# Dealing out the weight decoding, and moving a numerator copy, in linear attention with two MLPs

## The chip, the cores and the metric

The kernel runs on one core of one Trainium2 chip. The metric is device time in microseconds (us) of the whole launch; lower is better. Inputs are float32 (the MLP weights and alpha come as float64 and are split on the chip), and the output is float32.

## What is computed

```python
def phi(x):
    proj = np.einsum('bhsd,df->bhsf', x, w_phi)
    proj = proj - np.max(np.abs(proj), axis=-1, keepdims=True)
    return np.concatenate([np.exp(proj), np.exp(-proj)], axis=-1)
q_p, k_p = (phi(q), phi(k))
kv = np.einsum('bhsf,bhsd->bhfd', k_p, v)
z = np.sum(k_p, axis=2)
num = np.einsum('bhsf,bhfd->bhsd', q_p, kv)
den = np.einsum('bhsf,bhf->bhs', q_p, z)[..., None] + 1e-06
x = num / den                    # 4 batches, 8 heads, 576 tokens, 64 wide
h = x @ w_in1;  x = (h * np.cos(h)) @ w_out1
h = x @ w_in2;  x = (np.maximum(h, 0) + alpha * np.minimum(h, 0)) @ w_out2
```

The MLPs see 2304 tokens of 512 features, with 2048 hidden features.

## The kernel before, in words

**One order, written by hand.** The program is one list of steps, and every engine executes its instructions in the order in which the code issues them. Attention takes steps s = 0 to 50: eight groups n of four heads, five chunks of tokens each. In a step the tuple `order` calls its stages from top to bottom. The stages of a step work on different chunks: `project(s)` (TensorE, tile pj) makes the projections of key chunk s and of query chunk s - 2; `less_max` (VectorE, L460 and L464) takes the largest magnitude of a chunk and subtracts it; `k_exp` (ScalarE, L474) makes both exponentials of key chunk s - 1; `kv` (TensorE, L484) uses those of chunk s - 2; `q_transpose` (TensorE, L530, tile tp) and `q_exp` (ScalarE L549 and L563, GpSimd L565) make the query features as a high and a low part. This document counts steps by s, and calls s modulo 5 the remainder of the step.

**Numerators.** `num(n, pr, half, y)` multiplies query features by kv on TensorE (tile nm, L577) and copies the result out of PSUM in L583: with VectorE for y = 0, with ScalarE for y = 1. `NUM_AT` says in which step. Remainder 2, 3 and 4 have a numerator of either y, remainder 0 only one of y = 0, and remainder 1 only one of y = 1: that one is the lone numerator. nm and tp come in turn from one pool of two PSUM buffers, so a tile can only be written when the copy or the exponentials that read the tile two before it are done.

**Decoding.** The MLP weights are read as pairs of 32-bit words (`fetch_w`, two buffers ws) and turned into a high and a low float32r part by the ten instructions of `w_instructions`: ScalarE L118, L115 (the high part) and L129; VectorE L119, L123, L126, L127; GpSimd L132, L133, L134. The first five weights are decoded in attention (`w_some`, at the steps `W_AT`, parts spread by `W_PART`: L119 and L123 in the first step, L126 in the next, L127 after it). The others are decoded in the MLP steps k (`moe_step`), where a small planner picks the steps (`times`, `free`, `latest`, `decode_at`). MLP step k = -6 falls on s = 42, so the last attention steps and the first MLP steps share a time.

**MLP steps.** Step k computes one hidden tile (12 matmuls, ph), five steps ahead, and one output (12 matmuls, po) of a block of three or four hidden tiles; at the end of a block VectorE adds the four po tiles to acc (L236, L238), and only then the next block may write po. The last group of tokens has 256 tokens and two po tiles.

**Denominators.** `recip` sends a row to VectorE's layout and back through DRAM: transfers L592, L596 and L598 on SyncE's queue, `x_mult` (VectorE L605) uses what comes back, `x_split` (ScalarE L612, GpSimd L614) writes the MLP's input xh, xl.

Of the kernel before, what the change touches and what calls it, by code (L numbers as in the profile page):

```python
# [28 lines left out]
def feature_map_attention_two_mlps(  # L29
# [17 lines left out]
    NG4 = qT.shape[0]  # L47
# [46 lines left out]
    def w_instructions(spare=True):  # L94

        layer, which, ft, st = staged.pop(0)
        w_temps.append(w_temps.pop(0))
        u = w_temps[0].tile([P, DM], F32, tag="wu", name="wu")  # L100
        t = w_temps[0].tile([P, DM], I32, tag="wt", name="wt")
        e = w_temps[0].tile([P, DM], I32, tag="we", name="we")
        w0, w1 = st[:, :, 0], st[:, :, 1]
        tf, ef = t.bitcast(F32), e.bitcast(F32)
        ts, stt = nc.vector.tensor_scalar, nc.vector.scalar_tensor_tensor
        tt = nc.gpsimd.tensor_tensor
        tv, copy = (nc.vector.tensor_tensor, nc.vector.tensor_copy) if spare else (tt, nc.scalar.copy)
        hl = []

        def to_hi():  # L110
            hl.extend(w_tile(layer * NFT + ft, which, x) for x in "hl")
            w_t[layer, which, ft] = tuple(
                z.rearrange("p (k f) -> p k f", k=KD) if which == 0 else z for z in hl
            )
            copy(hl[0], tf)  # L115

        return [
            lambda: nc.scalar.activation(out=u, in_=w1.bitcast(F32), func=AF.Abs),  # L118
            lambda: ts(  # L119
                out=e, in0=w1, scalar1=0x07FFFFFF, scalar2=3, op0=ALU.bitwise_and,  # L120
                op1=ALU.logical_shift_left,
            ),
            lambda: stt(  # L123
                out=t, in0=w1, scalar=-0x40000000, in1=e, op0=ALU.bitwise_and, op1=ALU.bitwise_or
            ),
            lambda: stt(out=tf, in0=u, scalar=MIN_PATTERN, in1=tf, op0=ALU.is_ge, op1=ALU.mult),  # L126
            lambda: ts(out=e, in0=t, scalar1=-0x00800000, scalar2=None, op0=ALU.bitwise_and),  # L127
            to_hi,
            lambda: nc.scalar.activation(  # L129
                out=u, in_=w0.bitcast(U32), func=AF.Copy, scale=2.0 ** -52  # L130
            ),
            lambda: tt(out=u, in0=u, in1=ef, op=ALU.mult),  # L132
            lambda: tv(out=tf, in0=tf, in1=hl[0].bitcast(F32), op=ALU.subtract),  # L133
            lambda: tv(out=hl[1], in0=tf, in1=u, op=ALU.add),  # L134
        ]
# [17 lines left out]
    half_pi = const.tile([P, 1], F32, name="half_pi")  # L153
    al = const.tile([P, NFT], F32, name="al")
    h_t, g_t, o_t, pools = {}, {}, [], {}
    x_todo = []

    def mm3(ps, pairs, first=True, last=True):
        n = 3 * len(pairs)
        m = 0  # L160
        for (lh, ll), (rh, rl) in pairs:
            for l, r in ((lh, rh), (lh, rl), (ll, rh)):
                nc.tensor.matmul(ps, lhsT=l, rhs=r, start=(first and m == 0), stop=(last and m == n - 1))  # L163
                m += 1
# [50 lines left out]
    def output(j):  # L215
        layer, ft, g, fts = steps[j]
        c0, n = groups[g]
        gg = g_t.pop(j)
        ww = w_t[layer, 1, ft]
        nm = KD if layer == 0 else n // P  # L220
        w = n if layer == 0 else DM
        if ft == fts[0]:
            o_t[:] = [
                pools["ps_o"].tile([P, 512], F32, tag=f"po{m}", name=f"po{m}") for m in range(nm)
            ]
        for m in range(nm):
            s = slice(m * P, (m + 1) * P)
            l, r = (ww, gg) if layer == 0 else (gg, ww)
            mm3(o_t[m][:, 0:w], [((l[0][:, s], l[1][:, s]), r)], ft == fts[0], ft == fts[-1])
        if ft != fts[-1]:  # L230
            return
        for m in range(nm):
            po = o_t[m][:, 0:w]
            a = acc[g][:, m * w:(m + 1) * w]
            if fts[0] == 0:
                nc.vector.tensor_copy(a, po)  # L236
            else:
                nc.vector.tensor_tensor(out=a, in0=po, in1=a, op=ALU.add)  # L238
            if ft == NFT - 1:
                if layer == 0:  # L240

                    x_todo.append((xh[:, m, c0:c0 + n], xl[:, m, c0:c0 + n], a, nc.gpsimd))
                else:
                    nc.sync.dma_start(out=out[c0 + m * P:c0 + (m + 1) * P, :], in_=a)
# [21 lines left out]
    def reads(layer, which, ft):  # L266
        js = [j for j, st in enumerate(steps) if st[:2] == (layer, ft)]
        lead = LEAD_H - 1 if which == 0 else 0
        return js[0] - lead, js[-1] - lead

    w_all = []
    for i in range(2 * NFT):
        for which in range(2):
            w = (i // NFT, which, i % NFT)
            old = i - WSLOTS
            free = reads(old // NFT, which, old % NFT)[1] if old >= 0 else -1
            w_all.append((reads(*w)[0], free, w))
    w_all.sort(key=lambda w: w[0])
    w_seq = [w[2] for w in w_all[:len(EARLY)]]
# [1 line left out]
    def quiet(k):  # L281

        return (k < 0 or steps[k][1] != steps[k][3][-1]) and steps[k + LEAD][2] != NG - 1

    decode_at, at, todo = {}, -LEAD - 1, w_all[len(EARLY):]
    times = [t for t in range(1 - LEAD // 2, len(steps) - LEAD) if quiet(t)]
    latest = {}
    for need, free, w in reversed(todo):
        latest[w] = max(t for t in times if t < min([need - 2, *latest.values()]))
# [43 lines left out]
    with ExitStack() as actx:  # L333
# [286 lines left out]

        LAG = 2
        NUM_AT = (
            {5: (0, 0), 6: (0, 1), 7: (1, 0), 8: (1, 1)},
# [1 line left out]
        )  # L628
        NUM_LAST = 8
        KV_AT, KV_END, KV_LO = {5: (0,)}, {6: (1,)}, {5: (0,), 7: (1,)}  # L630
        W_AT = (7, 15, 23, 30, 37)
        W_PART = (0, 0, 0, 1, 2, 3, 3, 3, 4, 4)

        def num_step(n, pr, half, y):
            at = next(r for r, x in NUM_AT[y].items() if x == (pr, half))
# [17 lines left out]
                            f(n, pr, *a)  # L653
            return go

        w_run = []

        def w_some(s):
            if s in W_AT:
                w_run.extend(zip((s + d for d in W_PART), w_instructions(spare=False)))  # L660
            while w_run and s >= w_run[0][0]:
                w_run.pop(0)[1]()
                if not w_run:
                    fetch_w(*w_seq.pop(0))

# [7 lines left out]
        def group(f, table, lag, *a):  # L673
# [3 lines left out]
                        f(n, *table[s - lag - n * NC], *a)  # L677
            return go


        order = (
            group(kv_hi, KV_AT, 0),
            chunk(k_exp, -1, 0),
            chunk(kv, -2),
            nums_of(0),
            chunk(less_max, -LAG - 1, kind="q"),
            chunk(k_exp, -1, 1),
            nums_of(1),
            lambda s: kv_some(),
            group(kv_lo, KV_LO, 0),  # L690
            after(recip, 2, 2),
# [7 lines left out]
            chunk(q_exp, -LAG - 2, 1, True),  # L699
            after(x_split, 4, 5, False),  # L700
            after(x_split, 4, 5, True),
            w_some,
            chunk(less_max, 0, kind="k"),
        )


# [5 lines left out]
        for s in range(NS):  # L712
            if s + 3 < NK:
                load_x("k", s + 3)
                if s % NC == 2 and s // NC + 1 < NG4:
                    for pr in range(2):
                        load_v(s // NC + 1, pr)
            if 0 <= s - LAG + 3 < NK:
                load_x("q", s - LAG + 3)
            for stage in order:  # L720
                stage(s)
            if s < LAG:

                keep_warm(WARM)
            if s == 5:
                nc.sync.dma_start(
                    out=al, in_=alpha.rearrange("(f p) -> p f", p=P), allow_slow_non_contiguous=True
                )
            if s in (5, 7):
                fetch_w(*w_seq.pop(0))  # L730
            if s == S_H:
                kctx.close()
                pctx.close()
                pools["gp"] = ctx.enter_context(
                    tc.tile_pool(name="gp", bufs=LEAD + 1, reuse_waits="tile", side="right")
                )
                pools["mt"] = ctx.enter_context(
                    tc.tile_pool(name="mt", bufs=2, reuse_waits="tile", side="right")
                )
                pools["ps_h"] = ctx.enter_context(  # L740
                    tc.tile_pool(name="ps_h", bufs=4, space=PSUM, reuse_waits="tile")
                )
            if s == S_O:
                qctx.close()
                w_pools.append(ctx.enter_context(
                    tc.tile_pool(name="wpool2", bufs=1, reuse_waits="tile")
                ))
                w_temps.append(ctx.enter_context(
                    tc.tile_pool(name="wtmp2", bufs=1, reuse_waits="tile")
                ))  # L750
                pools["ps_o"] = ctx.enter_context(
                    tc.tile_pool(name="ps_o", bufs=1, space=PSUM, reuse_waits="tile", side="right")
                )
            if s >= S_H:
                assert not w_run and len(w_t) >= len(EARLY)
                moe_step(s - S_H - LEAD_H)
# [56 lines left out]
```

## Time and profile before

| what | value |
|---|---|
| median of 3 runs | 1007.64 us (1006.25 to 1009.91) |
| the profiled execution | 1009.28 us |
| its span, first to last instruction | 1007.1 us |
| mean granted TensorE clock | 0.993 |
| PE (matmul) busy | 985.2 us, 98% |
| DVE (VectorE) busy | 715.3 us, 71% |
| POOL (GpSimd) busy | 612.3 us, 61% |
| ACT (ScalarE) busy | 485.0 us, 48% |
| chain that ended last | PE 79%, DVE 11%, ACT 5%, issue 2%, DMA 1% |

A timeline row has its start, its length, the engine, the line, the operation, output<-input and the count; in brackets stands the idle time of that engine just before it, and what ended it. In a row of the waits stand the total, the number of waits and the longest. A windows row has its length, then the busy time of PE, PEld (weight loads), DVE, ACT and POOL with their instructions, the granted TensorE clock as a share of full speed, the DMA share and GB/s. PE's ends are modelled, so gaps in PE are read from the idle times, and lengths from start to start.

### The profile page before, as it was taken

Reading aid. Unit: us, or ns where it says so; the run is one execution under the profiler, and the core shown is the slowest. Engines: PE = TensorE matmul, PEld = TensorE weight load, DVE = VectorE, ACT = ScalarE, POOL = GpSimd, SP = SyncE. Lnnn points to the kernel's source line nnn. Section 1 sums busy time; section 2 is a strip of 40 time slices with the busy share of each in tenths; the row PEclk is TensorE's granted clock in tenths of the full one; section 3 lists DMA queues with packets and bytes.
Section 4 is the critical chain, followed back from the end, with each engine's and each line's share of the span. In section 5 each row is a group of like instructions: output and inputs, shape, how many; then the busy total and the mean of one; then the engine's idle time right before and its main releaser. Section 6 shows DMA issues by size and latency. Waiting matters only on the chain.

```text
span 1007.1 us, 14702 instructions
## 1 busy us (share of the span) xinstructions
PE 985.2 (98%) x5515; PEld 826.0 (82%) x5515; DVE 715.3 (71%) x1007; ACT 485.0 (48%) x935; POOL 612.3 (61%) x494
## 2 busy tenths in 40 slices
PE   9989989999999999999999999999999999999998
PEld 6988888877888888888888888888888888888887
DVE  5888878557785785885885788587749774976333
ACT  4868868775655654664656654223212321222000
POOL 2667768846474663663777789666636663676221
PEclk9989989999999999999999999999999999999999
DMA  6454443221020110110111111111101110110112
GB/s 155 131 134 130 116 138 95 65 68 43 21 64 22 63 42 21 63 42 21 63 63 43 31 54 43 42 43 56 50 21 42 63 44 21 42 63 1 42 42 105
DMA packets 64582, 60.67 MB, mean 60 GB/s; under 512 B 28928, under 2 KB 54656, under 8 KB 64512
## 3 DMA queue, kind: packets, MB, share of 16 engines
q1 hardware_dynamic: 64512, 59.75, 19.9%
q8 instruction: 43, 0.70, 0.3%
q14 instruction: 27, 0.22, 0.1%
HBM read 52.50 MB, written 4.79 MB: 57 GB/s over the span
## 4 chain that ended last, share of the span: by engine, by line
PE 79%; DVE 11%; ACT 5%; issue 2%; DMA 1%; POOL 1%; SPq 1%; ACTq 0%; DVEq 0%; POOLq 0%
PE po L163 34%; PE ph L163 33%; PE kv L484 4%; PE nm L577 4%; DVE wt L123 2%; PE pj L451 2%; DVE wt L126 2%; DVE we L119 1%; DVE r L190 1%; PE tp L530 1%; PE tp L416 1%; DVE acc L605 1%; DVE we L127 1%; DVE mx L460 1%; ACT r L193 1%
## 5 line engine op out<-in xcount | busy, mean ns | idle before, releaser
L86 POOL TENSOR_TENSOR gl<-r,gh 128x512 fp32r<-128x512 f32 (+1 forms) x160 | 207.5, 1298 | 274.2 <-ACT gh L85 255.2
L85 ACT CAST gh<-r 128x512 fp32r<-128x512 f32 (+1 forms) x160 | 92.0, 575 | 363.4 <-DVE r L209 260.5
L163 PE MATMUL ph<-xh,wil 128*128 128x512 f32 (+1 forms) x640 | 236.8, 370 | 0.1
L163 PE MATMUL ph<-xh,wih 128*128 128x512 f32 (+1 forms) x640 | 236.6, 370 | 0.0
L163 PE MATMUL ph<-xl,wih 128*128 128x512 f32 (+1 forms) x640 | 235.8, 368 | 0.0
L238 DVE TENSOR_TENSOR acc<-po,acc 128x512 f32<-128x512 f32 (+1 forms) x134 | 85.2, 656 | 75.6 <-PE po L163 75.2
L163 PEld LDWEIGHTS ph<-xl,wih 128*128 128x128 f32 x640 | 120.4, 188 | 22.1
L163 PEld LDWEIGHTS ph<-xh,wih 128*128 128x128 f32 x640 | 120.5, 188 | 21.9
L163 PEld LDWEIGHTS ph<-xh,wil 128*128 128x128 f32 x640 | 120.4, 188 | 21.8 <-POOL wil L134 0.5
L163 PE MATMUL po<-gh,wol 128*128 128x512 f32 (+1 forms) x320 | 119.5, 373 | 2.9 <-POOL wol L134 2.9
L163 PE MATMUL po<-gh,woh 128*128 128x512 f32 (+1 forms) x320 | 119.4, 373 | 1.9 <-DVE acc L236 1.4
L163 PE MATMUL po<-gl,woh 128*128 128x512 f32 (+1 forms) x320 | 118.9, 372 | 0.0
L163 PE MATMUL po<-woh,gh 128*128 128x512 f32 x288 | 113.9, 395 | 0.0
L163 PE MATMUL po<-wol,gh 128*128 128x512 f32 x288 | 113.7, 395 | 0.0
L163 PE MATMUL po<-woh,gl 128*128 128x512 f32 x288 | 113.5, 394 | 0.0
L132 POOL TENSOR_TENSOR wu<-wu,we 128x512 f32<-128x512 f32 x64 | 83.1, 1299 | 31.3 <-ACT wu L129 30.0
L123 DVE SCALAR_TENSOR_TENSOR wt<-ws,we 128x512 int32<-128x512 int32 x64 | 99.5, 1554 | 2.3
L196 DVE TENSOR_SCALAR r<-ph,al 128x512 f32<-128x512 f32 (+1 forms) x80 | 55.3, 691 | 58.5 <-PE ph L163 38.0
L126 DVE SCALAR_TENSOR_TENSOR wt<-wu,wt 128x512 f32<-128x512 f32 x64 | 79.4, 1241 | 8.8 <-ACT wu L118 4.9
L190 DVE SCALAR_TENSOR_TENSOR r<-r,ph 128x512 f32<-128x512 int32 (+1 forms) x80 | 50.3, 629 | 42.0 <-ACT r L182 40.7
L484 PEld LDWEIGHTS kv<-vm,kp 128*128 128x128 f32 x512 | 78.9, 199 | 0.8 <-ACT kp L474 0.4
L484 PE MATMUL kv<-vm,kp 128*128 128x66 f32 x512 | 79.3, 261 | 0.1
(80 smaller groups left out, 1834.2 us busy)
## 6 DMA issues: line engine op xcount, KB each, us to landing
ws<-in_moe_w_in_dram SPq DMA_DIRECT2D x32, 512.0 KB, 3.6
ws<-in_moe_w_out_dram SPq DMA_DIRECT2D x32, 512.0 KB, 3.4
acc<-dr SPq DMA_DIRECT2D x32, 144.0 KB, 3.0
out_dram<-acc SPq DMA_DIRECT2D x18, 256.0 KB, 2.1
vm<-in_v_dram SPq DMA_DIRECT2D x16, 256.0 KB, 3.8
kin<-in_k_dram SPq DMA_DIRECT2D x28, 128.0 KB, 2.9
qin<-in_q_dram SPq DMA_DIRECT2D x28, 128.0 KB, 2.9
acc<-acc SPq DMA_DIRECT2D x16, 144.0 KB, 2.8
```

Source lines behind the costliest of these rows:

```text
L85: nc.scalar.copy(hi, src)
L86: lo_engine.tensor_tensor(out=lo, in0=src, in1=hi.bitcast(F32), op=ALU.subtract)
L123: lambda: stt(out=t, in0=w1, scalar=-0x40000000, in1=e, op0=ALU.bitwise_and, op1=ALU.bitwise_or),
L126: lambda: stt(out=tf, in0=u, scalar=MIN_PATTERN, in1=tf, op0=ALU.is_ge, op1=ALU.mult),
L132: lambda: tt(out=u, in0=u, in1=ef, op=ALU.mult),
L163: nc.tensor.matmul(ps, lhsT=l, rhs=r, start=(first and m == 0), stop=(last and m == n - 1))
L190: nc.vector.scalar_tensor_tensor(out=r, in0=r.bitcast(I32), scalar=-2.0 * math.pi, in1=ph, op0=ALU.mult, op1=ALU.add)
L196: nc.vector.tensor_scalar(out=r, in0=ph, scalar1=0.0, scalar2=al[:, ft:ft + 1], op0=ALU.min, op1=ALU.mult)
L238: nc.vector.tensor_tensor(out=a, in0=po, in1=a, op=ALU.add)
L451: nc.tensor.matmul(pj[:, j, x, a], lhsT=xt[r, a * P:(a + 1) * P], rhs=w2[r], start=True, stop=True,)
L484: nc.tensor.matmul(kv_ps[pr][:, s, y * VW:(y + 1) * VW], lhsT=e[rows, s, 2 * a + y, :], rhs=v[rows], start=(c == (0, 2)[pr] and a == 0 and ...
L577: nc.tensor.matmul(nm, lhsT=l[:, s, pr, y * VW:(y + 1) * VW], rhs=r[:, s, y, :], start=(s == 0 and m == 0), stop=(s == 1 and m == 2),)
```

## The change

It has five parts. (1) In steps with the lone numerator (remainder 1) ScalarE copies the numerator first and makes the keys' exponentials after it (`exp_if`); other steps keep their order. (2) `less_max` of the keys moves ahead of `w_some`. (3) A decoding's VectorE operations are dealt out over steps of remainder 1, 3 and 4 (`W_STEPS`, `W_PARTS`): L119 in the first, L123 in the second, L126 with the cast L115 in the third, L127 with L129 and L132 in the fourth, L133 and L134 a step later. Decodings start at s = 6, 13, 21, 28, 36 instead of 7, 15, 23, 30, 37, and the first two fetches go out at s = 3 and 5 instead of 5 and 7. (4) The planner's first MLP steps: decodings at k = -2, 3, 4 instead of -1, 1, 3; the later ones stay. (5) In the last four outputs, the second po tile's matmuls of the first three are kept back and issued in the last.

```diff
+            o_todo[m].append(((l[0][:, s], l[1][:, s]), r))
+            if m == nm - 1 and ft != fts[-1] and j >= len(steps) - FB:
+                continue
+            mm3(o_t[m][:, 0:w], o_todo[m], len(o_todo[m]) + fts[0] > ft, ft == fts[-1])
...
-            free = reads(old // NFT, which, old % NFT)[1] if old >= 0 else -1
+            free = reads(old // NFT, which, old % NFT)[1] if old >= 0 else -LEAD
...
-    times = [t for t in range(1 - LEAD // 2, len(steps) - LEAD) if quiet(t)]
+    times = [t for t in range(2 - LEAD, len(steps) - LEAD) if quiet(t) and not 2 - LEAD < t < 3]
...
-        W_AT = (7, 15, 23, 30, 37)
-        W_PART = (0, 0, 0, 1, 2, 3, 3, 3, 4, 4)
+        W_STEPS = sorted(x + n * NC for n in range(NG4) for x in (6, 8, 9))
...
+        W_PARTS = ((0, 0, (0, 1)), (1, 0, (2,)), (2, 0, (3, 5)), (3, 0, (4, 6, 7)), (3, 1, (8, 9)))
...
+        def exp_if(first, half):
+            def go(s):
+                if first == any(num_step(n, pr, h, 0) == s for n in range(NG4) for pr in range(2) for h in range(2)):
+                    chunk(k_exp, -1, half)(s)
+            return go
...
-            chunk(k_exp, -1, 0),
+            exp_if(True, 0),
             chunk(kv, -2),
             nums_of(0),
             chunk(less_max, -LAG - 1, kind="q"),
-            chunk(k_exp, -1, 1),
+            exp_if(True, 1),
             nums_of(1),
+            exp_if(False, 0),
+            exp_if(False, 1),
...
+            chunk(less_max, 0, kind="k"),
             w_some,
-            chunk(less_max, 0, kind="k"),
...
-            if s in (5, 7):
+            if s in (3, 5):
                 fetch_w(*w_seq.pop(0))
```

What this moves shows best at three places. In the changed program all line numbers behind L440 or so are 6 or 7 higher: L467 and L471 are `less_max`, L590 the numerator's copy, L481 the keys' exponentials, L600 and L601 `recip`, L612 `x_mult`.

**VectorE, s = 15 and 16, before** (L605 is `x_mult` of s = 15, the copy L583 at the end belongs to s = 17):

```order
L605 TENSOR_TENSOR acc_81<-acc_81,acc_82 128x576
L119 TENSOR_SCALAR we<-ws 128x512
L123 SCALAR_TENSOR_TENSOR wt<-ws,we 128x512
L460 TENSOR_REDUCE mx<-pj 128x4
L464 TENSOR_TENSOR acc_80<-pj,mx 128x512
L460 TENSOR_REDUCE mx<-pj 128x4
L464 TENSOR_TENSOR acc_78<-pj,mx 128x512
L126 SCALAR_TENSOR_TENSOR wt<-wu,wt 128x512
```

The same stretch in the change, from s = 15 to the copy of s = 17:

```order
L612 TENSOR_TENSOR acc_81<-acc_81,acc_82 128x576
L467 TENSOR_REDUCE mx<-pj 128x4
L471 TENSOR_TENSOR acc_80<-pj,mx 128x512
L467 TENSOR_REDUCE mx<-pj 128x4
L471 TENSOR_TENSOR acc_78<-pj,mx 128x512
L467 TENSOR_REDUCE mx<-pj 128x4
L471 TENSOR_TENSOR acc_79<-pj,mx 128x512
L126 SCALAR_TENSOR_TENSOR wt<-wu,wt 128x512
L590 COPY acc_81<-nm 65x256
```

The two decoding operations that stood ahead of the keys' maxima of s = 15 are gone from there, and L126 now stands between the keys' maxima of s = 16 and the numerator copy of s = 17. L119 and L123 went to the ends of s = 13 and 14, each right ahead of the next step's copy:

```order
L471 TENSOR_TENSOR acc_80<-pj,mx 128x512
L119 TENSOR_SCALAR we<-ws 128x512
L590 COPY acc_80<-nm 65x256
L467 TENSOR_REDUCE mx<-pj 128x4
L471 TENSOR_TENSOR acc_78<-pj,mx 128x512
L467 TENSOR_REDUCE mx<-pj 128x4
L471 TENSOR_TENSOR acc_79<-pj,mx 128x512
L123 SCALAR_TENSOR_TENSOR wt<-ws,we 128x512
L590 COPY acc_80<-nm 65x320
```

**ScalarE, s = 16, before** (kp are the keys' exponentials, nm the lone numerator):

```order
L612 CAST xh<-acc_81 128x576
L118 ACTIVATE wu<-ws 128x512
L474 ACTIVATE kp<-acc_80 128x512 x2
L583 COPY acc_80<-nm 65x320
L518 CAST kvh<-kv_111 128x2x132
```

In the change:

```order
L619 CAST xh<-acc_81 128x576
L590 COPY acc_80<-nm 65x320
L481 ACTIVATE kp<-acc_80 128x512 x2
L525 CAST kvh<-kv_111 128x2x132
L556 ACTIVATE acc_78<-tp 128x256
```

The copy has passed the exponentials, and L118 of the decoding has left the step.

**SyncE, around MLP steps k = -3 to 1, before** (dr is the way through DRAM, ws a weight):

```order
L592 DMA acc_79<-acc_79 64x576
L596 DMA dr<-dn 128x9
L598 DMA acc_81<-dr 64x576 x2
L592 DMA acc_80<-acc_80 64x576
L596 DMA dr<-dn 128x9
L598 DMA acc_82<-dr 64x576 x2
L141 DMA ws<-in_moe_w_in_dram 128x4x256 x2
```

In the change:

```order
L599 DMA acc_79<-acc_79 64x576
L603 DMA dr<-dn 128x9
L605 DMA acc_81<-dr 64x576 x2
L141 DMA ws<-in_moe_w_in_dram 128x4x256
L599 DMA acc_80<-acc_80 64x576
L603 DMA dr<-dn 128x9
L605 DMA acc_82<-dr 64x576 x2
L141 DMA ws<-in_moe_w_in_dram 128x4x256
```

One weight's fetch has passed the last denominators' transfers.

## Rows read from the trace of the kernel before

**Rows 1.** Windows: seven stretches of five steps, from project(6) to project(41).

```profile
24.31:45.45 21.14, 20.87 (x220) 19.07 (x219) 17.41 (x33) 17.97 (x42) 13.25 (x15) 1.00 0.41 109
45.45:66.83 21.38, 21.04 (x220) 19.04 (x219) 17.95 (x31) 17.65 (x41) 17.39 (x17) 1.00 0.57 152
66.83:93.44 26.61, 23.68 (x219) 21.75 (x218) 21.00 (x37) 18.65 (x42) 17.95 (x17) 0.87 0.46 122
93.44:116.32 22.88, 21.11 (x219) 19.06 (x219) 19.73 (x37) 18.03 (x41) 16.53 (x16) 1.00 0.44 118
116.32:138.57 22.25, 21.00 (x219) 19.07 (x218) 18.42 (x33) 19.04 (x43) 18.61 (x18) 1.00 0.53 146
138.57:165.17 26.60, 23.67 (x220) 21.73 (x219) 21.00 (x37) 18.66 (x42) 17.95 (x17) 0.87 0.44 122
165.17:187.71 22.54, 20.89 (x212) 18.55 (x211) 19.60 (x37) 18.64 (x43) 16.29 (x16) 1.00 0.23 62
```

**Rows 2.** Waits of the whole span: engine, line <- releaser: total, times, longest.

```profile
PE nm L577 <- ACT acc L583: 8.4, 6, 2.7
...
PE po L163 <- POOL wol L134: 2.9, 2, 2.6
...
PE po L163 <- DVE acc L236: 1.4, 2, 0.9
```

**Rows 3.** Timeline, s = 15 to 17, the rows around PE's first long gap.

```profile
64.59 1.51 DVE L119 TENSOR_SCALAR we<-ws 128x512 int32<-128x512 int32 x1
...
66.13 1.65 DVE L123 SCALAR_TENSOR_TENSOR wt<-ws,we 128x512 int32<-128x512 int32 x1
...
69.14 1.15 ACT L474 ACTIVATE kp<-acc 128x512 f32<-128x512 f32 x2 [2.74 <-DVE acc L464]
...
70.19 0.40 ACT L583 COPY acc<-nm 65x320 f32<-65x320 f32 x1
...
70.65 0.48 PE L577 MATMUL nm<-qp0h,kvh 128*66 128x256 f32 x1 [2.66 <-ACT acc L583]
```

**Rows 4.** Windows of 1 us: one behind that gap.

```profile
75.00:76.00 1.00, 1.00 (x7) 1.00 (x7) 1.00 (x3) 0.00 (x0) 0.00 (x0) 0.50 1.10 244
```

**Rows 5.** Groups by form on VectorE, 66.8 to 165.2 us: busy, mean ns, idle before.

```profile
L123 DVE SCALAR_TENSOR_TENSOR wt<-ws,we 128x512 int32<-128x512 int32 x3 | 3.9, 1305 | 0.2
...
L119 DVE TENSOR_SCALAR we<-ws 128x512 int32<-128x512 int32 x2 | 1.9, 938 | 0.0
```

**Rows 6.** Timeline, s = 23 and the transposition of s = 24.

```profile
104.37 0.37 DVE L119 TENSOR_SCALAR we<-ws 128x512 int32<-128x512 int32 x1
...
104.77 0.69 DVE L123 SCALAR_TENSOR_TENSOR wt<-ws,we 128x512 int32<-128x512 int32 x1
...
107.24 0.66 PE L530 MATMUL tp<-ident,acc 128*128 128x128 f32 x4 [0.52 <-DVE acc L583]
```

**Rows 7.** Timeline (PE, ACT, SP), the page's DMA issues and the chain: first MLP steps.

```profile
227.51 0.50 PE L163 MATMUL po<-gh,wol 128*128 128x512 f32 x1 [2.57 <-POOL wol L134]
...
222.74 0.66 ACT L129 ACTIVATE wu<-ws 128x512 f32<-128x512 uint32 x1
...
210.45 0.54 SPq L592 DMA_DIRECT2D acc<-acc  x1
...
214.72 1.08 SPq L598 DMA_DIRECT2D acc<-dr  x2
223.43 12.25 SPq L141 DMA_DIRECT2D ws<-in_moe_w_in_dram  x2
...
acc<-dr SPq DMA_DIRECT2D x32, 144.0 KB, 3.0
...
309.10 2.74 PE ph L163 x12
311.84 2.79 PE po L163 x12
```

**Rows 8.** Timeline of VectorE, the end.

```profile
1002.85 1.39 DVE L238 TENSOR_TENSOR acc<-po,acc 128x512 f32<-128x512 f32 x2 [3.86 <-PE po L163]
```

More of the change, by code (lines that the diff above doesn't have):

```diff
@@ L155, in feature_map_attention_two_mlps @@
     h_t, g_t, o_t, pools = {}, {}, [], {}
+    o_todo = [[] for _ in range(KD)]
     x_todo = []
@@ L228, in output @@
             l, r = (ww, gg) if layer == 0 else (gg, ww)
-            mm3(o_t[m][:, 0:w], [((l[0][:, s], l[1][:, s]), r)], ft == fts[0], ft == fts[-1])
+            o_todo[m].append(((l[0][:, s], l[1][:, s]), r))
+            if m == nm - 1 and ft != fts[-1] and j >= len(steps) - FB:
+                continue
+            mm3(o_t[m][:, 0:w], o_todo[m], len(o_todo[m]) + fts[0] > ft, ft == fts[-1])
+            o_todo[m] = []
         if ft != fts[-1]:
@@ L654, in after @@
             return go
-        w_run = []
+        W_PARTS = ((0, 0, (0, 1)), (1, 0, (2,)), (2, 0, (3, 5)), (3, 0, (4, 6, 7)), (3, 1, (8, 9)))
+        w_run, w_free = [], [0]
         def w_some(s):
[L659 to L662, printed above, removed]
+            if not w_run and staged and len(w_t) < len(EARLY) and s in W_STEPS and s >= w_free[0]:
+                at = [x for x in W_STEPS if x >= s]
+                todo = w_instructions(spare=False)
+                w_run.extend((at[x] + d, [todo[y] for y in part]) for x, d, part in W_PARTS)
+                w_free[0] = at[3] + 2
+            while w_run and w_run[0][0] == s:
+                for f in w_run.pop(0)[1]:
+                    f()
                 if not w_run:
```

## The prediction, made before the changed kernel ran

> **What bounds the kernel now.** I read the windows first, then the waits, then the timeline around the longest of them. TensorE is busy nearly everywhere, so time can only come from stretches in which it does the same work more slowly or stands idle. The windows cut attention into stretches of five steps with the same work [rows 1]. The reader is to see that the first two take 21.14 and 21.38 us, the other five 26.61, 22.88, 22.25, 26.60 and 22.54, and that the two long ones alone have a mean clock of 0.87.
>
> The waits say why [rows 2]: TensorE waited 8.4 us, six times, for ScalarE's numerator copy L583, at most 2.7 us. The timeline shows such a wait from its root [rows 3]. VectorE did two decoding operations, 1.51 and 1.65 us, ahead of the keys' maxima of s = 15. ScalarE stood idle for 2.74 us for these maxima, then made the exponentials (1.15 us), and only then copied the lone numerator, which had long been ready. TensorE needed that buffer and idled for 2.66 us. Behind the gap it ran at a granted clock of 0.50, which is 1.2 GHz instead of 2.4 [rows 4]. So a long gap is paid about twice: a five-step stretch with one took 26.61 - 21.38 = 5.2 us more.
>
> In the MLPs nearly all is TensorE's own work. The waits there are 2.57 us in the output of k = 2 for a weight's low part wol [rows 7] and 1.4 us in two waits for the adds behind a block [rows 2], 4.0 us in all.
>
> **Part 1 to 3, attention: what goes.** If the five stretches from 66.83 to 187.71 us came down to 21.38 each, they would take 106.9 instead of 120.88 us: 13.98 us is the most that is to be had [rows 1]. The six waits for the copy lie at the six lone numerators that stand beside exponentials. The copy ahead of the exponentials makes it independent of the maxima; and with the maxima ahead of the decoding, and L119 and L123 gone from s = 15 and 30, the maxima are earlier too. I count these six waits, and both stretches at the lower clock, as gone.
>
> **What comes in their place.** The decoding's VectorE work stays the same, 20 operations; it now stands behind the keys' maxima, and so right ahead of the next step's numerator copy (the order excerpts of VectorE). The transposition on TensorE waits for that copy. One step of before shows the price [rows 6]: at s = 23 two operations, 0.37 + 0.69 = 1.06 us, made the transposition of s = 24 wait 0.52 us. About half a decoding operation's length in a step of remainder 3 therefore comes out as idle time. A single one has a mean of 0.94 (L119) or 1.31 us (L123) [rows 5], so 0.5 to 0.8 us each. Six operations land there (s = 13, 18, 23, 28, 33, 38): 3 to 5 us. Behind remainder 4 and 1 the next need is later; but L115 now stands on ScalarE behind L126 and ahead of the next exponentials, and what is queued behind it are the query exponentials that free the transposition's buffer. I estimate 0.5 us for each of five decodings, 2.5 us. The other bound: nothing comes back, since the operations fill idle time.
>
> A second working, by VectorE's load, checks this. Its idle time in a five-step stretch is 21.14 - 17.41 = 3.73, 3.43, 3.15, 3.83 and 2.94 us where no long gap stood [rows 1]: the queue's order does not let it go much below 3. The five stretches hold 99.75 us of VectorE work; with 2.94 us idle each they take 114.45 us, a gain of 6.4, and with 3.83 us 118.9, a gain of 2.0. The first working gives 13.98 less 5.5 to 7.5, so 6.5 to 8.5. I take 7.5 us, near the smaller idle time, because the change deals the work to steps where VectorE waited; the ends for the range are 2.0 and 13.98.
>
> The Trainium skill speaks against this part: "GPSIMD Engine Reference", section Specifications, says that GpSimd's SBUF interfaces are shared with VectorE, and that an instruction with two SBUF inputs or in a two-port mode contends for them. By that rule each of the dealt operations can meet a GpSimd operation of its own, and the sum would be that of the slower rival below. By the lengths of L119, 0.37 in one place and 1.51 in another [rows 3, 6], the trace agrees that it can happen.
>
> The fetches two steps earlier cost nothing as I see it: the weight's own 512 KB have no reader before s = 6, and no row shows TensorE idle for a load longer than the copies' waits; the first stretches are unchanged but for at most one dealt operation each.
>
> **Part 4, the first MLP steps.** The decoding that fed the 2.57 us wait stands one step earlier; a step is 2.74 + 2.79 = 5.5 us [rows 7], more than the wait, so it goes whole: -2.57. Two waits for the adds, 1.4 us, followed the decodings of k = 1 and 3. The one of k = 1 is gone; but k = 3 and 4 now decode in a row, ahead of the adds at k = 5, so the second stays or grows.
>
> The price is on SyncE's queue. The fetch behind this decoding may only start when L129 has read the buffer: before, it went out at 223.43, right behind L129 at 222.74 [rows 7]. Now it stands ahead of the last denominators' transfers (the excerpt of SyncE), and these wait behind it. Before, they took from 210.45 to 214.72 + 1.08 + 3.0 = 218.8, 8.35 us [rows 7]. With L129 at most 5.5 us earlier, at 217.2, the fetch leaves no earlier than about 217.9, and they end at 226 or later, with the weight's 512 KB ahead of them up to 2 us later. VectorE's multiplication by them (L605) stands ahead of two more operations and of the adds of the block that ends with k = 2; at some 0.7 us each (1.39 for two adds [rows 8]) the first add is then done between 229 and 231, later still if L129 is less than 5.5 us earlier. That block's matmuls end near 227.51 + 2.5 - 2.57 = 227.4 (2.5 is what was left of 2.79 at the wait), and a hidden tile of 2.74 us covers TensorE until 230.2. So it stands for 0 to 3 us at k = 3; I take 1.5, and as much at k = 6, where the hidden tile in between has only 256 tokens and covers half as long. New waits 3.0 against old 4.0: a gain of 1.0 us, with ends of a loss of 2.5 and a gain of 3.5.
>
> **Part 5, the end.** VectorE's two last adds run from 1002.85 to 1004.24 without a gap [rows 8]: the second starts when the first ends, and TensorE's last matmul ends there too. Keeping back the second tile's matmuls starts the first add earlier and leaves the second, and the last transfer, where they were. I count zero; at most the second transfer shares the engines with the first no more, a few tenths.
>
> **Sum.** 7.5 + 1.0 + 0 = 8.5 us off. The profiled execution took 1009.28 us, so 1000.8 on its scale; the median of the runs is 1007.64, 1.6 us lower, and on its scale it is 999.1. I give the latter. About 0.3%, 3 us, is what a measurement of this kernel can tell from no change.
>
> **Rivals.**
>
> *The waits go and nothing comes back* (0.20). For it: two stretches with a decoding part did run at 21.14 and 21.38 us [rows 1]. Against it: VectorE would have to be busy 99.75 of 106.9 us. Attention gives 14, the MLPs 3.5: 990.
>
> *Moved, not removed* (0.20). The lone copy is early, but ScalarE's next work, the query exponentials behind the keys', is as late as the keys' maxima, and TensorE waits for that buffer instead; VectorE keeps an idle time of 3.8 us a stretch. For it: 8.4 us less twice 2.66 leaves 3.1 us of such waits for four steps [rows 2, 3], and one of them, at s = 21, has no decoding operation on VectorE from s = 18 to 22, so the queue itself is late there. Attention gives 2, the MLPs 1 or lose 1: 1005 to 1007.
>
> *Slower: every dealt operation pays alone* (0.10). VectorE operations stretch beside GpSimd's: L119 took 0.37 in one place and 1.51 in another [rows 3, 6]. Before, two in a row shared one such delay. If 14 operations that stand ahead of a copy each take their long time and 1.2 us of it shows, 16.8 us come back against 13.98 taken, and the transfers behind the fetch add 2.5: 1013. It decides from about 1 us for each of these operations on.
>
> The forecast has 0.50, its own range 995 to 1003.5.
>
> **How the numbers follow.** Faster by over 0.3% is below 1004.6: nearly all of the forecast (0.48), all of the first rival (0.20) and a quarter of the second (0.05), 0.73 in all. Slower by over 0.3% is above 1010.7: the third rival, 0.08 of its 0.10, and little else, 0.08. Within 0.3% is left with 0.19. The range reaches from just below the first rival's time, 989, to the upper end of the second, 1007; it leaves out the third and the first one's lower tail.
>
> **What would show it.** Right: no wait of TensorE over 2 us in attention and no second with a clock of 0.50 between 60 and 190 us; the waits for the numerator copy on ScalarE near zero; five-step stretches of 21.5 to 23 us; new waits of the transposition for the copy on VectorE, 3 to 5 us in all, at the steps with remainder 3; no wait for wol; SyncE's last denominator transfers leaving after the fetch, and a wait of the first outputs of k = 3 or 6 for the adds. Wrong: stretches still above 24 us, or a gap of 2.5 us with the lower clock at another step; or stretches at 21.4, which would mean that I charged the dealt operations for nothing.

## The result and the profile after

The changed kernel takes **1020.1 us** in the median of four runs (1016.79 to 1022.11), the kernel before 1006.94 in the same comparison (1004.55 to 1009.91). The ratio is 1.0126 with a 95% interval of 1.0087 to 1.0165: slower by 1.3%, where 999.1 was forecast. The profiled execution is the shortest of the four: 1016.79 us, span 1014.4 at a mean clock of 0.991. Against the span of before, 1007.1, that is 7.3 us more. In the other three the mean clock was 0.983 to 0.986.

The five-step windows of the changed kernel stand at other times than before, but hold the same steps, project(6) to project(41):

```profile
24.95:49.41 24.46, 22.61 (x220) 20.52 (x219) 18.23 (x32) 17.50 (x41) 13.26 (x14) 0.93 0.28 73
49.41:71.50 22.09, 21.03 (x219) 19.05 (x218) 18.29 (x32) 17.36 (x40) 17.27 (x17) 1.00 0.54 147
71.50:99.41 27.91, 25.03 (x219) 22.35 (x218) 22.36 (x39) 19.98 (x45) 18.74 (x19) 0.88 0.43 119
99.41:122.60 23.19, 21.33 (x220) 19.14 (x219) 19.04 (x35) 17.77 (x42) 13.55 (x15) 1.00 0.44 113
122.60:144.97 22.37, 21.26 (x219) 19.22 (x218) 19.97 (x33) 17.93 (x42) 19.77 (x18) 1.00 0.52 145
144.97:170.99 26.02, 23.23 (x220) 20.61 (x219) 21.68 (x36) 18.85 (x43) 18.32 (x18) 0.93 0.47 125
170.99:196.09 25.10, 22.80 (x211) 20.30 (x210) 20.94 (x38) 19.24 (x45) 14.83 (x15) 0.93 0.20 55
```

Every stretch but the sixth became longer, the first by 24.46 - 21.14 = 3.3 us [rows 1]. Together they went from 163.40 to 171.14 us: **+7.7, the whole loss**. The start costs 0.6 more, and from project(41) to the end there are 818.3 us instead of 819.4, which gives the 7.3. Four stretches instead of two now run partly at the lower clock.

By the kind of step (seven of each, changed kernel less before): remainder 1 (lone numerators) **-7.6**; remainder 3 **+9.65**; remainder 4 **+5.6**; remainders 2 and 0 +0.1 together.

TensorE's waits in the changed kernel (total, times, longest):

```profile
PE tp L537 <- DVE acc L590: 9.2, 8, 1.6
PE po L164 <- ACT r L194: 3.3, 2, 1.7
...
PE kv L491 <- ACT kp L481: 1.7, 3, 0.6
...
PE nm L584 <- ACT acc L590: 1.1, 2, 0.6
```

The wait that was to go did: the copy on ScalarE is waited for 1.1 us instead of 8.4 [rows 2]. In its place the transposition waits 9.2 us, eight times, for the copy on VectorE. The timeline of the changed kernel at s = 18 shows one such wait, VectorE and GpSimd together:

```profile
83.96 2.51 POOL L572 TENSOR_TENSOR qp1l<-acc,qp1h 128x512 fp32r<-128x512 f32 x2
...
84.77 0.69 DVE L471 TENSOR_TENSOR acc<-pj,mx 128x512 f32<-128x512 f32 x1
...
85.38 1.38 DVE L127 TENSOR_SCALAR we<-wt 128x512 int32<-128x512 int32 x1
...
86.68 0.41 DVE L590 COPY acc<-nm 65x256 f32<-65x256 f32 x1
...
87.15 0.66 PE L537 MATMUL tp<-ident,acc 128*128 128x128 f32 x4 [1.31 <-DVE acc L590]
```

L127 took 0.42 us at four of its five places in the kernel before. Here it starts while GpSimd makes the low half of the query features (L572, until 86.47) and is done only behind it, after 1.38 us. The copy stands right behind it, and TensorE idles 1.31 us for the copy. The maxima's subtraction L471, beside the same GpSimd work, keeps its 0.69 us.

All seven steps of remainder 3 have a dealt operation in this place (s = 8 to 38), five beside L572 like this one, the two L119 (s = 13 and 28) mostly beside the decoding's own L134. Their lengths are 1.78, 0.98, 1.38, 1.79, 1.05, 1.53 and 1.78 us, **10.29 in all**; the steps grew by **9.65**. Behind three of these gaps (before 38.76, 87.15 and 185.88), and behind two waits of 0.6 us at s = 31, the clock falls. Two windows of 1 us: one behind the gap before 38.76, at the lower clock, and one behind a gap as long (1.59 us, before 113.23), at the full clock:

```profile
41.00:42.00 1.00, 1.00 (x9) 0.78 (x8) 0.15 (x1) 0.58 (x2) 1.00 (x2) 0.50 0.00 0
...
114.00:115.00 1.00, 1.00 (x20) 1.00 (x21) 0.49 (x1) 1.00 (x3) 0.00 (x0) 1.00 0.79 229
```

The 5.6 us at remainder 4 are steps 9, 19 and 39 at the lower clock (+1.55, +2.69, +1.32).

In the first MLP steps the 2.57 us for wol [rows 7] are gone and 3.3 us stand in two new waits. The rows of the timeline (SyncE, VectorE, TensorE):

```profile
227.93 0.39 SPq L141 DMA_DIRECT2D ws<-in_moe_w_in_dram  x1
...
229.01 0.54 SPq L603 DMA_DIRECT2D dr<-dn  x1
...
233.02 1.09 SPq L605 DMA_DIRECT2D acc<-dr  x2
...
236.51 0.76 DVE L612 TENSOR_TENSOR acc<-acc,acc 128x576 f32<-128x576 f32 x1 [1.95 <-DMA acc<-dr]
...
239.11 2.48 DVE L242 COPY acc<-po 128x512 f32<-128x512 f32 x4
...
239.94 0.47 PE L164 MATMUL po<-gh,woh 128*128 128x512 f32 x1 [1.71 <-ACT r L194]
...
243.15 1.67 DVE L123 SCALAR_TENSOR_TENSOR wt<-ws,we 128x512 int32<-128x512 int32 x1
...
247.80 1.67 DVE L123 SCALAR_TENSOR_TENSOR wt<-ws,we 128x512 int32<-128x512 int32 x1
...
254.44 0.47 PE L164 MATMUL po<-gh,woh 128*128 128x512 f32 x1 [1.59 <-ACT r L194]
```

The last denominators' transfers leave behind the fetch and VectorE's multiplication L612 waits for them, as worked out. The first wait follows from that: ScalarE's cast of the product (until 237.99) holds up L183, L183 holds up VectorE's L191, and L194 and the copies L242, which empty the po tiles, come behind it. Ahead of the second wait two decodings stand in a row, 243.15 and 247.80.

### The profile page after: what moved, and what is told of

It is laid out like the page before. It is cut to its first block, busy times and chain, and to the rows that moved or that the text cites. A ratio compares the mean times of both kernels' runs of the same rounds, so it can differ in the third digit from the quotient of the medians.

```text
span 1014.4 us, 14711 instructions
## 1 busy us (share of the span) xinstructions
PE 990.9 (98%) x5515; PEld 829.3 (82%) x5515; DVE 719.7 (71%) x1007; ACT 484.6 (48%) x935; POOL 610.0 (60%) x494
## 4 chain that ended last, share of the span: by engine, by line
PE 82%; DVE 10%; ACT 4%; issue 2%; DMA 1%; POOL 1%; SPq 0%; DVEq 0%; ACTq 0%; POOLq 0%
PE po L164 34%; PE ph L164 34%; PE kv L491 5%; PE nm L584 4%; PE pj L458 3%; DVE wt L123 2%; PE tp L537 2%; DVE wt L126 1%; DVE r L191 1%; DVE we L127 1%; DVE mx L467 1%; PE tp L423 1%; DVE we L119 1%; ACT r L183 1%; ACT r L194 1%
## 5 line engine op out<-in xcount | busy, mean ns | idle before, releaser
L123 DVE SCALAR_TENSOR_TENSOR wt<-ws,we 128x512 int32<-128x512 int32 x64 | 101.7, 1589 | 2.1
L132 POOL TENSOR_TENSOR wu<-wu,we 128x512 f32<-128x512 f32 x64 | 82.9, 1296 | 31.0 <-ACT wu L129 29.1
L126 DVE SCALAR_TENSOR_TENSOR wt<-wu,wt 128x512 f32<-128x512 f32 x64 | 79.1, 1237 | 8.9 <-ACT wu L118 5.4
L191 DVE SCALAR_TENSOR_TENSOR r<-r,ph 128x512 f32<-128x512 int32 (+1 forms) x80 | 50.3, 628 | 43.2 <-ACT r L183 41.7
```

Of the source, the lines that this page charges most:

```text
L123: lambda: stt(out=t, in0=w1, scalar=-0x40000000, in1=e, op0=ALU.bitwise_and, op1=ALU.bitwise_or),
L191: nc.vector.scalar_tensor_tensor(out=r, in0=r.bitcast(I32), scalar=-2.0 * math.pi, in1=ph, op0=ALU.mult, op1=ALU.add)
```

## The experiments

Every run is named here by the first part of its label (e1 to e12) and compared with the kernel before on its own chip; there the median of before was 1009.75 (first four runs), 1007.6 (next four), 1008.5 (next three) and 1009.22 us (the last). Steps are compared as above. Theory P is that the place ahead of the numerator copy makes a dealt operation cost.

### Dealt operations behind the copy (e1_behind)

```diff
-                for f in w_run.pop(0)[1]:
-                    f()
+                for y, f in w_run.pop(0)[1]:
+                    if s % NC == 3 and y in (1, 2, 4, 7):
+                        held.append(f)
+                    else:
+                        f()
...
             nums_of(0),
+            w_held,
```

> The changed kernel, but a VectorE operation dealt to a step of remainder 3 is issued behind the next step's numerator copy instead of ahead of it; all else as in the change. Theory P (the place: the copy waits for the operation, the transposition for the copy): the seven waits of the transposition at remainder 3, about 9 us in the changed kernel, fall below 2 us, the falls of the clock behind them go too, and the span is 998 to 1004 us. Rival L (load: VectorE has no room left in attention, so the operations cost their length wherever they stand): the wait turns up at another tile or step, and the span stays at 1010 us or more.

**997.66 us**, ratio 0.9887 (0.9872 to 0.9901), clock 1.00 throughout. The steps of remainder 3 are 0.7 us below before, attention takes 152.37 us instead of 163.40. The timeline at s = 18 again:

```profile
78.13 2.52 POOL L572 TENSOR_TENSOR qp1l<-acc,qp1h 128x512 fp32r<-128x512 f32 x2
...
79.54 0.41 DVE L590 COPY acc<-nm 65x256 f32<-65x256 f32 x1
...
79.87 1.06 DVE L127 TENSOR_SCALAR we<-wt 128x512 int32<-128x512 int32 x1
...
80.00 0.66 PE L537 MATMUL tp<-ident,acc 128*128 128x128 f32 x4
```

L127 is still stretched, and the seven operations still take 7.88 us; but the copy is ahead of it and TensorE doesn't wait. (GpSimd's L132, which uses what L127 makes, went behind the copy with it.) At remainder 3 the length alone costs nothing; in front of the copy it does. What is left are 1.9 us at the steps of remainder 0, behind the operations dealt to remainder 4.

### One part at a time (e2_copy_only, e3_max_only, e4_mlp_only)

The kernel before with part 1 alone (`exp_if`):

> The kernel before with the lone numerator's copy ahead of the keys' exponentials, nothing else. If the copy's place behind the exponentials is what made the long gaps, both gaps of 2.66 us and the low clock behind them go, as do the three waits of 1 us: span about 1007 - 12 = 995 us. If ScalarE is late for another reason (the cast of x_split stands ahead of the copy and waits for VectorE's multiplication, and the query exponentials behind it are as late as the keys' maxima), the gaps only shrink: span 1000 to 1004 us.

1004.15 us, ratio 0.9943 (0.9921 to 0.9965): remainder 1 falls by 4.3 us, nothing else moves by over 0.5. The gaps only shrink. At s = 16 and 31, 9.07 and 8.08 us long, TensorE now waits for the keys' exponentials, which stand behind the late maxima, and the clock still falls:

```profile
70.28 0.44 PE L484 MATMUL kv<-vm,kp 128*128 128x66 f32 x2 [1.56 <-ACT kp L474]
```

Part 2 alone:

```diff
+            chunk(less_max, 0, kind="k"),
             w_some,
-            chunk(less_max, 0, kind="k"),
```

> The kernel before with the keys' maxima issued ahead of the step's decoding, nothing else: decodings at s = 7, 15, 23, 30, 37, with L119 and L123 in one step. Theory P: the gaps at s = 16 and 31 go (the maxima are no longer behind two decoding operations), but at s = 23 the two operations now stand right ahead of the copy that the transposition waits for, so the step grows from 5.3 to about 7 us; span 998 to 1004 us. Rival L: no gain, span 1006 us or more.

1016.77 us, ratio 1.0067 (1.0047 to 1.0088): **slower by itself**. Of the two expectations only rival L's time fits, and its reason is ruled out by e1. Remainder 1 gains 6.2 us, but remainders 2, 3 and 4 lose 3.2, 5.2 and 4.8, and not at s = 23 (5.72 us where 7 were expected) but at s = 8 and 38, with the lower clock behind. Before, L126 of s = 8 ran in 0.68 us ahead of the maxima. Now (timeline, GpSimd, VectorE, TensorE):

```profile
36.75 2.52 POOL L565 TENSOR_TENSOR qp1l<-acc,qp1h 128x512 fp32r<-128x512 f32 x2 [2.92 <-ACT qp1h L563]
...
38.03 1.78 DVE L126 SCALAR_TENSOR_TENSOR wt<-wu,wt 128x512 f32<-128x512 f32 x1
...
40.20 0.66 PE L530 MATMUL tp<-ident,acc 128*128 128x128 f32 x4 [1.59 <-DVE acc L583]
```

Parts 4 and 5 alone:

> The kernel before with the change's MLP parts alone: decodings at k = -2, 3, 4 and the second po tile of the last outputs kept back. From the two traces, the stretch from project(41) to the end went from 819.4 to 818.3 us, so a span of about 1006 us, within 0.2% of the kernel before; the wait for wol is gone and two waits of 1.6 us at the first outputs stand in its place.

1008.94 us, ratio 0.9989 (0.9972 to 1.0005): no difference that this measurement can tell, the forecast 1.0 us being within it.

### The change without part 2 (e5_max_behind)

```diff
-            chunk(less_max, 0, kind="k"),
             w_some,
+            chunk(less_max, 0, kind="k"),
```

> The changed kernel with part 2 undone: the keys' maxima of a step stand behind its decoding operation again, everything else stays. Theory O (the order of maxima and decoding is what costs: ahead of the maxima the operation runs while VectorE waits for the projection, behind them it stands right ahead of the next numerator copy): the steps of remainder 3 come back to 4.6 to 5.0 us each, no transposition waits over 0.7 us, 1000 to 1006 us. Rival D (a dealt operation at remainder 3 delays the next copy on either side of the maxima, so the dealing itself costs): remainder 3 stays at 5.6 to 6.5 us a step, 1015 to 1021 us.

**998.72 us**, ratio 0.9908 (0.9886 to 0.9930), below the range of theory O. One moved line takes back 21 us. The same L127 of s = 18, now ahead of the maxima:

```profile
78.81 0.37 DVE L127 TENSOR_SCALAR we<-wt 128x512 int32<-128x512 int32 x1
79.10 0.69 DVE L467 TENSOR_REDUCE mx<-pj 128x4 f32<-128x512 f32 x1
...
80.50 0.41 DVE L590 COPY acc<-nm 65x256 f32<-65x256 f32 x1
```

It is done in 0.37 us, begun 0.2 us before GpSimd's next L572, and the maxima behind it lose little. Remainder 3 is 2.3 us above before instead of 9.65. Not all of it went as expected: the transposition still waits 3.6 us in seven places, up to 1.0 where 0.7 was the bound, and the steps 13 and 28 stay at 5.5 and 5.7 us, where L119 takes 1.33 us beside the decoding's L133 and pushes the maxima and the copy back.

### Another remainder (e6_rem0)

```diff
-        W_STEPS = sorted(x + n * NC for n in range(NG4) for x in (6, 8, 9))
+        W_STEPS = sorted(x + n * NC for n in range(NG4) for x in (6, 9, 10))
```

> The changed kernel with the decodings dealt to the steps of remainder 1, 4 and 0 where the change has 1, 3 and 4 (one number in the table); the order inside a step stays. The step behind remainder 0 has no numerator copy on VectorE. Theory P (place): the extra 9.65 us at remainder 3 and the 5.6 us behind them at the lower clock go, 1001 to 1007 us. Rival C (each operation is stretched beside GpSimd and pays wherever it stands): the delays appear at remainder 1 instead, 1013 to 1021 us.

1011.17 us, ratio 1.0035 (1.0016 to 1.0054): between the two, and neither theory as put. Remainder 3 is back (0.8 us below before), but remainder 1 is at 45.12 us, as long as before. At s = 26 (timeline, VectorE, ScalarE, TensorE, and one window of 1 us behind it):

```profile
116.11 1.48 DVE L126 SCALAR_TENSOR_TENSOR wt<-wu,wt 128x512 f32<-128x512 f32 x1
...
117.62 0.62 ACT L115 CAST wih<-wt 128x512 fp32r<-128x512 f32 x1 [2.06 <-DVE wt L126]
...
118.15 0.41 ACT L590 COPY acc<-nm 65x320 f32<-65x320 f32 x1
...
118.61 0.33 PE L584 MATMUL nm<-qp0h,kvh 128*66 128x256 f32 x1 [3.23 <-ACT acc L590]
...
120.00:121.00 1.00, 1.00 (x7) 1.00 (x7) 0.64 (x2) 1.00 (x7) 0.60 (x2) 0.50 0.58 138
```

The place that was free on VectorE wasn't free on ScalarE: the decoding's cast L115 waits for L126 ahead of the lone copy, and a gap of 3.23 us returns. Rival C is not wholly wrong either: at s = 31 the transposition waits 1.45 us for VectorE's copy. The step was chosen by one queue and failed in another.

### Copy and maxima without the dealing (e8_copy_max)

> The kernel before with parts 1 and 2 alone: the lone copy ahead of the exponentials, the keys' maxima ahead of the decoding, which stays in two pieces of several operations. Theory P: the two places at which part 2 alone lost (s = 8 and 38, 4.7 us each with the lower clock behind) stay lost, and s = 16 and 31 come to about 5.1 us each instead of 9.9: 1005 to 1010 us. Rival (the dealing is what hurts, the first two parts are good together): 996 to 1001 us.

1014.45 us, ratio 1.0068 (1.0047 to 1.0088), above the range given: s = 16 and 31 came to 6.6 us each where 5.1 was expected, and beside s = 9 and 39 the step s = 32 lost 1.6 us at the lower clock too. Part 2 costs about 10 us beside part 1 as well (1004.15 without it), so it does harm without the dealing.

### GpSimd out of the way (e9_gp_free)

```diff
+                    if c != 4:
                         nc.gpsimd.tensor_tensor(out=dl, in0=et, in1=dh.bitcast(F32), op=ALU.subtract)
...
+                    elif s == 1:
+                        for dl, et, dh in low:
+                            nc.scalar.copy(dl, et)
```

> The changed kernel with GpSimd's two subtractions for the low halves of the last query chunk of each group (L572, 2.5 us at the steps of remainder 3) left out; ScalarE writes those buffers with two plain copies instead, so this part of the computation (the low halves of the query features of that chunk) is missing. VectorE's order is that of the changed kernel. Theory G (the dealt operation at remainder 3 is as long as GpSimd's subtraction lets it be, and its stretched length is what the transposition waits): L123 falls from 1.8 to 0.7 us and L127 from 1.4 to 0.4 us there, the seven steps of remainder 3 grow by 3 to 5 us instead of 9.65, little of the lower clock is left, 1004 to 1010 us. Rival (place alone, whatever the length): lengths and waits stay, 1016 to 1022 us.

1005.25 us, ratio 0.9976 (0.9959 to 0.9992), with VectorE's order of the changed kernel. GpSimd and VectorE at s = 18:

```profile
79.81 1.43 POOL L630 TENSOR_TENSOR xl<-acc,xh 128x576 fp32r<-128x576 f32 x1
...
83.13 0.42 DVE L127 TENSOR_SCALAR we<-wt 128x512 int32<-128x512 int32 x1
...
83.47 0.41 DVE L599 COPY acc<-nm 65x256 f32<-65x256 f32 x1
...
84.43 1.27 POOL L132 TENSOR_TENSOR wu<-wu,we 128x512 f32<-128x512 f32 x1 [3.19 <-ACT wu L129]
```

L127 is back at 0.42 and L123 at 0.68 us; L119, beside the decoding's own L134, stays at 1.0. Remainder 3 is 3.5 us above before, remainder 4 level with it. So of the 9.65 us about 3.5 are the place, with operations mostly of their plain length, and about 6 the stretching; the 5.6 us at remainder 4 are the clock behind. Four cases side by side, sums over the seven steps of remainder 3:

```
                                  operations' length   growth of the steps
changed kernel                          10.29                +9.65
behind the copy (e1)                     7.88                -0.70
ahead of the maxima (e5)                 5.34                +2.25
GpSimd's L572 left out (e9)              4.93                +3.54
```

### The first outputs (e7_fetch_later, e10_mixed, e11_max_behind_k, e12_mixed_k)

e7 is e1 with the fetch one step later:

```diff
-            if w_seq:
+            if w_seq and k != 2 - LEAD:
                 fetch_w(*w_seq.pop(0))
+        if k == 3 - LEAD:
+            fetch_w(*w_seq.pop(0))
```

> As the run with the operations behind the copy (997.66 us), and the fetch of k = -2 is issued one step later, behind the last denominators' transfers in SyncE's queue. Theory Q (the two waits at the first outputs of k = 3 and 6, 3.3 us, come from these transfers standing behind the fetch): both waits fall below 0.5 us, 994 to 995.5 us. Rival: they come from the decodings of k = 3 and 4 that stand in a row ahead of the adds; the waits stay, 997 to 998.5 us.

997.33 us, ratio 0.9895 (0.9872 to 0.9918), as the rival had it. TensorE's two waits there, and VectorE ahead of the second:

```profile
220.99 0.47 PE L164 MATMUL po<-gh,woh 128*128 128x512 f32 x1 [0.83 <-ACT r L194]
...
232.41 1.40 DVE L127 TENSOR_SCALAR we<-wt 128x512 int32<-128x512 int32 x1
...
233.73 0.68 DVE L208 TENSOR_TENSOR r<-ph,r 128x512 f32<-128x512 f32 x1
...
234.66 2.47 DVE L242 COPY acc<-po 128x512 f32<-128x512 f32 x4
...
235.48 0.47 PE L164 MATMUL po<-gh,woh 128*128 128x512 f32 x1 [1.62 <-ACT r L194]
```

The transfers had made half of the first wait (1.75 in e1). The second is not theirs. Followed back, it leads to the second of the two decodings: its L126 and L127, 1.33 and 1.40 us long, stand right ahead of L208, for which ScalarE sat idle for 3.17 us, and of the copies L242, which empty the po tiles. The changed kernel has the same rows (L126 1.32, L127 1.41 us). e10 adds a mixed order to e7 (`w_some` called twice, ahead of the maxima at remainder 4 and for L126 at remainder 1) and the decodings k = -2, 1 and 3:

```diff
+            lambda s: w_some(s, True),
             chunk(less_max, 0, kind="k"),
             w_some,
...
-... quiet(t) and not 2 - LEAD < t < 3]
+... quiet(t) and t not in (-1, 0, 2)]
```

> The run with the operations behind the copy and the later fetch (997.33 us), with the dealt operation ahead of the keys' maxima at remainder 4 and, for L126, at remainder 1, and with the first MLP decodings at k = -2, 1 and 3. Theory: the steps of remainder 0 behind them come back by 0.5 us each, s = 16 and 31 by 0.6 us each, and the second wait at the first outputs, 1.6 us, goes, since no two decodings stand in a row any more: 993.5 to 995.5 us. Rival (other waits take their place, as the adds of before did with 1.4 us): 996.5 to 998.5 us.

997.51 us, ratio 0.9908 (0.9882 to 0.9935). Attention came to 150.48 us, 1.9 less than in e7 where the expectation adds up to 2.7; the MLPs gave it back in one wait, with the lower clock behind it. Ahead of it stand the decoding of k = 1 on VectorE, four operations from 214.47 to 217.91, and behind these the multiplication by the denominators:

```profile
214.47 1.52 DVE L119 TENSOR_SCALAR we<-ws 128x512 int32<-128x512 int32 x1
...
221.25 0.47 PE L164 MATMUL po<-gh,woh 128*128 128x512 f32 x1 [3.02 <-ACT r L194]
```

e11 has the same planner and fetch over e5:

> The changed kernel without part 2 (998.72 us), with the later fetch and the first MLP decodings at k = -2, 1 and 3. Attention as in that run. If the decodings of k = 3 and 4 in a row make the second wait and the transfers the first, the 3.3 us of waits at the first outputs fall below 1.5 us: 996 to 997.5 us. If they only move: 998 to 999.5 us.

998.69 us, ratio 0.9918 (0.9892 to 0.9945), with the same wait of 3.02 us: the waits only moved. So e12 takes e10's attention with the changed kernel's own k = -2, 3 and 4:

> The mixed run (997.51 us; its attention steps 6 to 40 took 150.48 us, and a wait of 3.0 us with the lower clock behind it stood at the first outputs) with the changed kernel's own first MLP decodings at k = -2, 3 and 4. If the terms add up: 150.5 us for the attention steps, 817.9 us from there to the end as in the run with the later fetch, 994 to 996 us. If the attention steps' gain is taken back in the MLPs: 997 to 998 us.

**995.15 us, ratio 0.9865 (0.9848 to 0.9881)**, the best version: 150.41 us of attention, full clock throughout. Two waits of together 2.4 us at the first outputs are left. That the second hangs on a decoding is read from the rows; that it needs two decodings in a row is not shown, since the runs with k = 1 and 3, where it is absent, changed several things there at once.

## Why the prediction was wrong

**The step that failed** is the price of the dealt operations, "About half a decoding operation's length ... 0.5 to 0.8 us each. Six operations land there ... 3 to 5 us". It took the half from one step of before, in which two short operations (1.06 us) made a wait of 0.52 [rows 6]; half of 0.94 and 1.31 would be 0.5 to 0.7. They stood ahead of the maxima, where VectorE waits for the projection and a part of their time costs nothing. Behind the maxima no idle time is left before the copy, as at s = 8 of the changed kernel:

```profile
35.18 0.69 DVE L467 TENSOR_REDUCE mx<-pj 128x4 f32<-128x512 f32 x1 [1.11 <-PE pj L458]
...
36.59 1.78 DVE L123 SCALAR_TENSOR_TENSOR wt<-ws,we 128x512 int32<-128x512 int32 x1
...
38.29 0.41 DVE L590 COPY acc<-nm 65x256 f32<-65x256 f32 x1
```

So 9.65 us showed of operations that take 10.29, over seven instead of six: s = 8 was not counted, and the first stretch, taken as unchanged, grew by 3.3 us. Of before's lengths the mean was taken [rows 5], though the places differ: behind the maxima they meet GpSimd's 2.5 us of L572, ahead of them mostly nothing. With mostly plain lengths (e9) 3.5 us came out, inside the forecast; the stretching made it 9.65.

**What follows from it** was not priced either: gaps of 1.3 to 1.6 us were followed by the lower clock, +5.6 us at remainder 4 in the profiled execution; the other three, 3 to 5 us longer, have lower mean clocks. "Both stretches at the lower clock" were counted as gone; the one behind s = 16 went, the one at s = 31 stayed, and three came. The sum of 9.65 and 5.6 is 15.2 against the 5.5 to 7.5 allowed for all that comes back.

**The sign of part 2** was wrong. The maxima ahead of the decoding was read as an earlier release of the exponentials. That is real (remainder 1 gains 6.2 us in e3), but part 1 alone with the dealing makes the copy independent of the maxima anyway (e5: 33.0 us at remainder 1, where e1 has 33.0 too). Part 2 thus brought nothing beside part 1, and moved the operations to the one place that TensorE waits on.

**The gain** of 13.98 us was the right size: e12 takes 150.41 us for attention, 13.0 less than before. In the changed kernel only 7.6 us of it came at the lone numerators, where e1 and e5 gain 12.1 and 12.2, so that some 4.5 stayed where 2.5 were allowed for what ScalarE's queue brings: at s = 16 and 31 there are still waits of 0.6 us each for the copy and the keys' exponentials, and part of s = 31 runs at the lower clock.

**VectorE's load as a check** pointed to a smaller gain, but for the wrong reason, and this was luck: it holds idle time constant, and so says nothing of where in a step the work stands. e1 and the changed kernel have nearly the same VectorE work in these stretches (137.2 and 140.5 us) and differ by 18.8 us.

**The rival that came nearest** is "every dealt operation pays alone", at 0.10: the sign fits, and so does the stretching beside GpSimd. But not every operation paid. The seven at remainder 3 paid 1.4 us each, where it had 1.2 for 14; at remainder 4 L123 took 1.58 us at s = 14 and 29, and these steps kept their 3.75 us. It lacked the clock too, so its 1013 us is near for partly wrong reasons. The range, 989 to 1007, left it out.

It draws on what the Trainium skill says in "GPSIMD Engine Reference", section Specifications: GpSimd's SBUF interfaces are shared with VectorE, and instructions with two SBUF inputs or in a two-port mode contend. The runs agree: L123, with two such inputs, takes 1.78 us beside L572 and 0.68 without it (e9), and L471, which reads one input from PSUM, keeps 0.69 us beside it. That the shared interface is the cause was not tried by itself; that L572 is what stretches them was.

**MLP and end** held in the sum: -1.1 us from project(41) on against -1.0. The 2.57 us went whole; the new waits are 3.3 us where 3.0 were allowed. But the second was put down to the transfers, and e7 shows that it hangs on a decoding, so that half of this sum is luck.

**The list of what would show it** named waits of the transposition for VectorE's copy at remainder 3 as the new cost, and that is the line which now leads.

## What to carry to other kernels

Price moved work by where it lands: what it is queued ahead of, how much idle time lies before that, and which other engine runs at that moment; a mean of lengths over all places hides the last two. Work that nobody waits for goes behind the instruction that others wait for, not ahead of it; on an in-order queue that was worth 22 us here for seven short operations, the clock included. And check every queue that a piece of work uses: VectorE's free step was ScalarE's busy one.

## What was unexpected of the hardware

- A decoding operation of VectorE that starts beside a GpSimd operation is not slowed by a factor but held until that one ends: L123 took 1.78, 1.79 and 1.78 us at s = 8, 23 and 38 of the changed kernel, where GpSimd's pair of 2.52 us had begun 1.3 us earlier, and 1.46, 1.45 and 1.46 us in e1, where it started later, and each time it ended 0.55 us behind GpSimd; it took 0.68 us without the pair (e9). So did the four L123 at s = 14 and 29 of both runs (1.25 to 1.58 us). L119 and L127 ended 0.28 or 0.29 us behind the GpSimd operation beside them in 19 of 20 cases of the two runs. How long such an operation takes is thus set by when it starts. Operations that read PSUM ran beside it at their usual 0.63 to 0.69 us.
- Gaps of the same length are followed by the lower clock or aren't: 1.58 us before 38.76 was, 1.59 before 113.23 was not; the two waits of 0.6 us were at s = 31 and not at s = 16. What decides was not tried.
- The spread shows it too: the four executions of the changed kernel lie 5.3 us apart with mean clocks of 0.983 to 0.991, those of e1, at 0.999 and 1.00, 1.0 us.
